# Linear attention plus SwiGLU on one core: tile 2 transposed by DMA, tile 0 normalised on ScalarE, and a new order of the first tiles

## The chip, the core and the metric

The kernel runs on one core of one Trainium2 chip. Time is device microseconds of one execution. The engines are named as in the profile: PE (TensorE, matrix multiplication), ACT (ScalarE), DVE (VectorE), POOL (GpSimd) and SP (SyncE, which here only issues DMAs). Each engine works through its own list in order and waits at semaphores for the others. A DMA is issued by SP or ACT and runs on the core's DMA engines.

## The reference, cut to what matters

S = 2048 rows, D = 512, F = 1792, 32 heads of 16, all tensors bf16.

```python
xn = layernorm(x)                                  # no scale or shift, eps 1e-5
q, k, v = split(xn @ wqkv)                         # 32 heads of 16
phi = lambda t: where(t > 0, t + 1, exp(t)) + 1e-6
kv = sum_s phi(k) v^T;  z = sum_s phi(k)           # per head
attn = (phi(q) kv) / (phi(q) z + 1e-6) @ wo
ffn = (silu(xn @ w_gate) * (xn @ w_up)) @ w_down
out = x + attn + ffn
```

The attention has no softmax. The kernel never forms v: it accumulates GT = xn^T phi(k) over all rows, and multiplies it by V's weights afterwards.

## The kernel before, in words

The 2048 rows are 16 tiles of 128. The kernel has two long stages. The first goes over the tiles: statistics of x, normalisation, a transpose of xn, the products with K's and Q's weights, phi(k), and the accumulation of GT in PSUM banks 4 to 7 (`gtacc`, four matmuls of 128x512 per tile). The second goes over 4 chunks of 512 rows times 14 slices of F (`ffn`), with the output rows (`outtile`) in between. K's product of tile t goes to bank 0 or 2, Q's to bank 1 or 3, by whether t is even.

The order of the work is written out by hand: `K.op` appends an instruction to the list of its engine, `K.dma` a transfer to the list of SP or ACT, and the waits follow from the names that each reads and writes. So the place of a line in the source is its place in its engine's list, and in no other.

Tiles 0 to 2 are treated apart, to start PE early. They are only centred (`xc_half`, DVE, two halves of 256 columns), transposed on PE (`tp_first`, two 128x128 transposes per half, evacuated to `xcT` by ACT at line 382), multiplied with K's and Q's weights (`proj_first`, in halves of two matmuls), and scaled by rstd only as ACT reads the products: `first_ek` (exp), `first_pk` (relu), `first_pq` (copy). For these tiles phi(k) is the sum of a clipped exponential and the relu, on POOL for tile 0 (`feat_pool`) and on DVE for tiles 1 and 2 (`first_feat`). GT needs the normalised rows as well, which `xn_dve` makes on DVE. The mean of tile 0 comes from DVE (`bns` and `agg`), that of tile 1 from ACT (`mean_act`, an activation whose sum is read out). Before the first tile, `fill` gives PE eight matmuls on a constant.

From tile 3 on, `xn_dve` makes xn, SP transposes it by DMA (`transpose_dma`), and `kproj` and `qproj` read the result.

`eps` and `rstd_of` make 1/sqrt(var + eps) from the variance, the second always on POOL. SP's list holds the loads of x, of the weights and the DMA transposes in one queue; at the start ACT issues three loads, too: x 1, one of four chunks of K's weights, and x 2.

Of the kernel before, what the change touches and what calls it, by code (L numbers as in the profile page):

```python
# [7 lines left out]
ALU = mybir.AluOpType  # L8
# [100 lines left out]
def bass_parallel_sum__linear_attn_block__swiglu_ffn__prompt_kernel(  # L109
# [16 lines left out]
    with contextlib.ExitStack() as es:  # L126
# [75 lines left out]
        def xload(eng, h, t0, n, after=()):  # L202
            K.dma(
                eng, lambda: h.dma_start(x_sb[:, t0:t0 + n, :], rows(xin, t0, n)),
                r=list(after), w=[("x", t0 + i) for i in range(n)],
            )

        def wqkv_load(eng, h, name, i, c0, n, after=()):
            K.dma(
                eng,  # L210
                lambda: h.dma_start(
                    wqkv_sb[:, c0:c0 + n, i * D:(i + 1) * D],
                    A_wqkv[c0 * P:(c0 + n) * P, i * D:(i + 1) * D].rearrange("(c p) f -> p c f", p=P),
                ),
                r=list(after), w=[(name, c) for c in range(c0, c0 + n)],
            )
# [32 lines left out]
        wqkv_load("sp", sp, "wk", 1, 0, 2)  # L249
        wqkv_load("act", act, "wk", 1, 3, 1)  # L250
        wqkv_load("sp", sp, "wk", 1, 2, 1)
        xload("act", act, 2, 1)
        xload("sp", sp, 3, 1)
        wqkv_load("sp", sp, "wq", 0, 0, 1)
        wqkv_load("sp", sp, "wq", 0, 1, 1)
        wqkv_load("sp", sp, "wq", 0, 2, 1)
        wqkv_load("sp", sp, "wq", 0, 3, 1)
        xload("sp", sp, 4, 1)
        xload("sp", sp, 5, 1)
        xload("sp", sp, 6, 2)  # L260

        cw = nc.const_aps.tensor(1.0, (P, P), bf)
        cx = nc.const_aps.tensor(1.0, (P, 512), bf)
# [1 line left out]
        def fill(n, cols, after=()):  # L265
            K.op(
                "pe",
                [
                    (lambda: pe.matmul(banks[3][:, 0:cols], cw, cx[:, 0:cols], start=True, stop=True))
                    for _ in range(n)  # L270
                ],
                r=list(after), w=[bk(3)],
            )
# [22 lines left out]
        def bns(t):  # L296
            K.op("dve", lambda: dve.bn_stats(stats[:, t, :], x_sb[:, t, :]), r=[("x", t)], w=[("st", t)])  # L297

        def agg(t):
            K.op("dve", lambda: dve.bn_aggr(mv[:, t, :], stats[:, t, :]), r=[("st", t)], w=[("mv", t)])  # L300

        def mean_act(t):
            K.op(
                "act",
                lambda: act.activation(
                    scr[:, :], x_sb[:, t, :], ACT.Copy, scale=1.0 / D, accum_out=mact[:, t, :],
                ),
                r=[("x", t)], w=[("mact", t), ("scr",)],
            )

        def xn_dve(t):
            K.op(
                "dve",
                lambda: dve.tensor_scalar(
                    out=xn_sb[:, t, :], in0=x_sb[:, t, :], scalar1=mv[:, t, 0:1], scalar2=rstd[:, t:t + 1],
                    op0=ALU.subtract, op1=ALU.mult,
                ),
                r=[("x", t), ("mv", t), ("rstd", t)], w=[("xn", t)],
            )

        def eps(t, eng):
            h = dve if eng == "dve" else pool
            K.op(
                eng,
                lambda: h.tensor_scalar(
                    out=vpe[:, t:t + 1], in0=mv[:, t, 1:2], scalar1=1e-5, scalar2=None, op0=ALU.add,
                ),
                r=[("mv", t)], w=[("vpe", t)],
            )

        def rstd_of(t):
            K.op(
                "pool",
                lambda: pool.tensor_tensor(out=rstd[:, t:t + 1], in0=vpe[:, t:t + 1], in1=nhalf[:, :], op=ALU.pow),
                r=[("vpe", t), ("nhalf",)], w=[("rstd", t)],
            )
# [19 lines left out]
        def xc_half(t, h, mean=None, dep="mv"):  # L356
            mean = mv[:, t, 0:1] if mean is None else mean

            K.op(
                "dve",  # L360
                lambda: dve.tensor_scalar(  # L361
                    out=xc_sb[:, t, h * HD:(h + 1) * HD], in0=x_sb[:, t, h * HD:(h + 1) * HD],
                    scalar1=mean, scalar2=None, op0=ALU.subtract,
                ),
                r=[("x", t), (dep, t)], w=[("xc", t, h)],
            )

        def tp_first(t, h, b):
            tb = banks[b].bitcast(bf)[:, 0:HD].rearrange("p (c s) -> p c s", c=2)
            K.op(  # L370
                "pe",
                [
                    (lambda c=c: pe.transpose(  # L373
                        tb[:, c, :], xc_sb[:, t, (2 * h + c) * P:(2 * h + c + 1) * P], ident[:, :],
                    ))
                    for c in range(2)
                ],
                r=[("xc", t, h), ("ident",)], w=[bk(b)],
            )
            K.op(  # L380
                "act",
                lambda: act.activation(xcT[:, NDC * t + 2 * h:NDC * t + 2 * h + 2, :], tb, ACT.Copy),  # L382
                r=[bk(b)], w=[("xcT", t, h)],
            )
# [22 lines left out]
        def proj_first(t, wname, h):  # L407
            lo, b = (D, kb(t)) if wname == "wk" else (0, qb(t))
            K.op(
                "pe",  # L410
                [
                    (lambda c=c: pe.matmul(  # L412
                        banks[b], xcT[:, NDC * t + c, :], wqkv_sb[:, c, lo:lo + D],
                        start=(c == 0), stop=(c == NDC - 1),
                    ))
                    for c in (2 * h, 2 * h + 1)
                ],
                r=[("xcT", t, h)] + [(wname, i) for i in ((2, 3) if h else (0, 1))], w=[bk(b)],
            )
# [55 lines left out]
        def first_pk(t):  # L475
            K.op(
                "act", lambda: act.activation(kpos[:, t, :], banks[kb(t)], ACT.Relu, scale=rstd[:, t:t + 1]),
                r=[bk(kb(t)), ("rstd", t)], w=[("kpos", t)],
            )
# [27 lines left out]
        def clip_k(t):  # L507
            clip(ek[:, t % NE, :], ("ek", t % NE))
# [47 lines left out]
            if t >= 3:  # L556
                transpose_dma(t)

        bns(0)
        mean_act(1)  # L560
        fill(8, 512)
        agg(0)
        eps(0, "pool")
        xc_half(0, 0)
        tp_first(0, 0, 4)
        xc_half(0, 1)
        tp_first(0, 1, 5)
        fill(1, P)
        xc_half(1, 0, mact[:, 1, :], "mact")
        tp_first(1, 0, 6)  # L570
        xc_half(1, 1, mact[:, 1, :], "mact")
        tp_first(1, 1, 7)
        bns(1)
        proj_first(0, "wk", 0)
        proj_first(0, "wk", 1)
        rstd_of(0)
        first_ek(0)
        first_pk(0)
        xn_dve(0)
        agg(1)  # L580
        eps(1, "pool")
        rstd_of(1)
        proj_first(1, "wk", 0)
        proj_first(1, "wk", 1)
        bns(2)
        proj_first(1, "wq", 0)
        first_ek(1)
        proj_first(0, "wq", 0)
        agg(2)
        xc_half(2, 0)  # L590
        tp_first(2, 0, 4)
        xc_half(2, 1)
        tp_first(2, 1, 5)
        clip_k(0)
        feat_pool(0)
        bns(3)
        agg(3)
        eps(3, "dve")
        rstd_of(3)
        bns(4)  # L600
        agg(4)
        proj_first(0, "wq", 1)
        first_pq(0)
        xn(3)
        xload("sp", sp, 8, 2)
        clip_k(1)
        xn_dve(1)
        proj_first(1, "wq", 1)
        first_pk(1)
        first_feat(1)  # L610
        first_pq(1)
        eps(4, "pool")
        rstd_of(4)
        xn(4)
        xload("sp", sp, 10, 2)
        bns(5)
        agg(5)
        eps(2, "pool")
        rstd_of(2)
        proj_first(2, "wk", 0)  # L620
        proj_first(2, "wk", 1)
        first_ek(2)
        clip_k(2)
        eps(5, "dve")
        rstd_of(5)
        xn_dve(2)
        first_pk(2)
        first_feat(2)
        proj_first(2, "wq", 0)
        proj_first(2, "wq", 1)  # L630
        first_pq(2)
        xn_dve(5)
        bns(6)
        agg(6)
        eps(6, "pool")
        gtacc(0)
        gtacc(1)
        kproj(3)
        exp_k(3)
        clip_k(3)  # L640
        maxadd_k(3)
        transpose_dma(5)
        xload("sp", sp, 12, 2)
        qproj(3)
        copy_q(3)
        exp_q(3)
        gtacc(2)
        rstd_of(6)
        zsum(0, 0)
        xn(6)  # L650
        xload("sp", sp, 14, 2)
        bns(7)
        agg(7)
        kproj(4)
        bns(8)
        exp_k(4)
        eps(7, "pool")
        rstd_of(7)
        qproj(4)
        exp_q(4)  # L660
        copy_q(4)
        clip_k(4)
        agg(8)
        eps(8, "pool")
        rstd_of(8)
        zsum(1, 1)
        maxadd_k(4)
        xn(7)
        stat(9)
        gtacc(3)  # L670

# [331 lines left out]
```

## Time and profile before

| | us |
|---|---|
| median of 3 runs | 211.75 (211.21 to 211.9) |
| the profiled execution | 211.24 |
| its span | 210.0 |
| PE busy | 206.7 |
| DVE busy | 119.9 |
| POOL busy | 74.3 |
| ACT busy | 70.2 |

The span runs from the first to the last recorded instruction; the profiled execution's own time has 1.24 us around it. Busy times are sums over instructions; matmuls are pipelined, so a matmul of 128x512 has a mean duration of 379 ns in the records though the next may start sooner. In a row of the timeline stand start, length, engine, line, operation, output and input, the count of merged instructions, and in brackets the idle time before the first with what ended it. A time to landing is from the issue of a DMA to its completion.

### The profile page before, as it was taken

Reading aid. Unit: us, or ns where it says so; the run is one execution under the profiler, and the core shown is the slowest. Engines: PE = TensorE matmul, PEld = TensorE weight load, DVE = VectorE, ACT = ScalarE, POOL = GpSimd, SP = SyncE. Lnnn points to the kernel's source line nnn. Section 1 sums busy time; section 2 is a strip of 40 time slices with the busy share of each in tenths; the row PEclk is TensorE's granted clock in tenths of the full one; section 3 lists DMA queues with packets and bytes.
Section 4 is the critical chain, followed back from the end, with each engine's and each line's share of the span. In section 5 each row is a group of like instructions: output and inputs, shape, how many; then the busy total and the mean of one; then the engine's idle time right before and its main releaser. Section 6 shows DMA issues by size and latency. Waiting matters only on the chain.

```text
span 210.0 us, 2773 instructions
## 1 busy us (share of the span) xinstructions
PE 206.7 (98%) x987; PEld 94.7 (45%) x987; DVE 119.9 (57%) x245; ACT 70.2 (33%) x124; POOL 74.3 (35%) x95
## 2 busy tenths in 40 slices
PE   7999999999999999999999999999999999999996
PEld 3444444445444444444444444444444444444444
DVE  3999998336265774647365746365556535374122
ACT  5876666956643331302122312213031213121000
POOL 3647997668032444222140432230424032221200
DMA  6666365696792011110202110202021010110201
GB/s 192 207 144 163 70 95 102 193 372 218 211 351 44 10 29 26 35 25 28 50 2 50 25 28 25 50 0 50 3 50 25 25 25 30 43 33 27 50 25 53
DMA packets 29743, 16.71 MB, mean 80 GB/s; under 512 B 20384, under 2 KB 29088, under 8 KB 29728
## 3 DMA queue, kind: packets, MB, share of 16 engines
q1 hardware_dynamic: 29296, 16.13, 28.9%
q10 hardware_dynamic: 432, 0.39, 0.6%
q8 instruction: 8, 0.13, 0.3%
q14 instruction: 7, 0.06, 0.1%
HBM read 9.70 MB, written 2.10 MB: 56 GB/s over the span
## 4 chain that ended last, share of the span: by engine, by line
PE 96%; DMA 1%; DVE 1%; ACT 0%; issue 0%
PE psum L723 46%; PE psum L906 23%; PE psum L398 11%; PE psum L895 7%; PE psum L539 7%; PE psum L412 2%; DMA x_sb<-in_A_x_dram 1%; ACT xcT L382 0%; PE psum L821 0%; PE psum L844 0%; DVE stats L297 0%; PE psum L373 0%; DVE xc_sb L361 0%; DVE out_sb L919 0%; DVE mv L300 0%
## 5 line engine op out<-in xcount | busy, mean ns | idle before, releaser
L738 ACT ACTIVATE sg<-psum 128x512 bf16<-128x512 f32 x56 | 33.4, 598 | 106.8 <-PE psum L723 103.8
L723 PE MATMUL psum<-xnT,wu_sb 128*128 128x512 bf16 x224 | 57.5, 379 | 0.0
L723 PE MATMUL psum<-xnT,wg_sb 128*128 128x512 bf16 x224 | 57.5, 379 | 0.0
L853 POOL TENSOR_TENSOR prod<-pkq,zb 128x512 f32<-128x512 bf16 x16 | 18.6, 1162 | 57.7 <-DVE pkq L463 57.7
L723 PEld LDWEIGHTS psum<-xnT,wu_sb 128*128 128x128 bf16 x224 | 21.9, 98 | 26.4
L723 PEld LDWEIGHTS psum<-xnT,wg_sb 128*128 128x128 bf16 x224 | 21.9, 98 | 26.2
L919 DVE TENSOR_TENSOR out_sb<-psum,x_sb 128x512 bf16<-128x512 f32 (+2 forms) x17 | 11.2, 660 | 36.2 <-PE psum L906 36.2
L877 POOL TENSOR_TENSOR pqn<-pkq,rden 128x512 bf16<-128x512 bf16 x16 | 16.9, 1055 | 36.6 <-DVE rden L871 36.6
L744 DVE TENSOR_TENSOR pkq<-psum,sg 128x512 bf16<-128x512 f32 x28 | 19.1, 687 | 18.5 <-PE psum L723 14.1
L744 DVE TENSOR_TENSOR xn_sb<-psum,sg 128x512 bf16<-128x512 f32 x28 | 18.8, 671 | 13.8 <-PE psum L723 12.2
L906 PE MATMUL psum<-wd_sb,xn_sb 128*128 128x512 bf16 (+2 forms) x126 | 25.7, 355 | 0.0
L906 PE MATMUL psum<-wd_sb,pkq 128*128 128x512 bf16 x112 | 25.5, 379 | 0.0
L398 PE MATMUL psum<-wqkv_sb,xnT 128*128 128x512 bf16 x104 | 24.4, 379 | 0.0
L531 POOL TENSOR_TENSOR zacc<-zacc,pkq 128x512 f32<-128x512 f32 x15 | 17.3, 1155 | 4.9 <-DVE ek L454 4.6
L906 PEld LDWEIGHTS psum<-wd_sb,xn_sb 128*128 128x128 bf16 x126 | 11.8, 98 | 12.4
L906 PEld LDWEIGHTS psum<-wd_sb,pkq 128*128 128x128 bf16 x112 | 11.0, 98 | 13.2
L895 PE MATMUL psum<-m_sb,eq 128*128 128x512 bf16 (+2 forms) x68 | 16.6, 367 | 0.0
L539 PE MATMUL psum<-pkq,xn_sb 128*128 128x512 bf16 x64 | 15.9, 379 | 0.0
L398 PEld LDWEIGHTS psum<-wqkv_sb,xnT 128*128 128x128 bf16 x104 | 10.1, 98 | 12.4 <-issue 0.5
L861 DVE TENSOR_REDUCE den<-prod 128x32 f32<-128x512 f32 x16 | 10.9, 684 | 5.7 <-POOL prod L853 5.7
L297 DVE BATCH_NORM_STATS2 stats<-x_sb 128x6 f32<-128x512 bf16 x16 | 10.9, 683 | 3.3 <-DMA x_sb<-in_A_x_dram 3.3
L463 DVE SCALAR_TENSOR_TENSOR pkq<-pkq,eq 128x512 bf16<-128x512 bf16 x16 | 11.1, 692 | 0.6
(62 smaller groups left out, 137.4 us busy)
## 6 DMA issues: line engine op xcount, KB each, us to landing
out_dram<-out_sb SPq DMA_DIRECT2D x15, 128.0 KB, 1.7
wg_sb<-in_B_w_gate_dram SPq DMA_DIRECT2D x2, 896.0 KB, 7.9
wu_sb<-in_B_w_up_dram SPq DMA_DIRECT2D x2, 896.0 KB, 6.0
wd_sb<-in_B_w_down_dram SPq DMA_DIRECT2D x1, 1792.0 KB, 9.8
x_sb<-in_A_x_dram SPq DMA_DIRECT2D x5, 256.0 KB, 2.9
wqkv_sb<-in_A_wqkv_dram SPq DMA_DIRECT2D x5, 128.0 KB, 3.9
x_sb<-in_A_x_dram SPq DMA_DIRECT2D x4, 128.0 KB, 3.4
wqkv_sb<-in_A_wqkv_dram SPq DMA_DIRECT2D x1, 512.0 KB, 7.9
```

Source lines behind the costliest of these rows:

```text
L398: (lambda c=c: pe.matmul(banks[b], xnT[:, c, t * P:(t + 1) * P], wqkv_sb[:, c, lo:lo + D], start=(c == 0), stop=(c == NDC - 1),))
L463: lambda: dve.scalar_tensor_tensor(out=dst, in0=src, scalar=0.0, in1=e, op0=ALU.max, op1=ALU.add,),
L531: lambda: pool.tensor_tensor(out=zacc[:, :], in0=zacc[:, :], in1=pk, op=ALU.add),
L539: (lambda c=c: pe.matmul(banks[4 + c], xn_sb[:, t, c * P:(c + 1) * P], pkq[:, t, 0, :], start=(t == 0), stop=(t == NT - 1),))
L723: (lambda c=c: pe.matmul(banks[b], w_sb[:, c, fc * P:(fc + 1) * P], xnT[:, c, C * 512:(C + 1) * 512], start=(c == 0), stop=(c == NDC - 1),))
L738: lambda: act.activation(sg[:, j % NSG, :], banks[gb], ACT.Silu),
L744: lambda: dve.tensor_tensor(out=hT(C, fc), in0=banks[ub], in1=sg[:, j % NSG, :], op=ALU.mult,),
L853: lambda: pool.tensor_tensor(out=p, in0=pkq[:, t, 1, :], in1=zb[:, :], op=ALU.mult),
L877: lambda: pool.tensor_tensor(out=pqn[:, t % NPN, :].rearrange("p (h e) -> p h e", e=DH), in0=pkq[:, t, 1, :].rearrange("p (h e) -> p h e", ...
L895: (lambda g=g: pe.matmul(dst, pqnT(t)[:, g, :], m_sb[:, g, lo:hi], start=(g == 0), stop=False,))
L906: (lambda fc=fc: pe.matmul(dst, hT(C, fc)[:, jj * P:(jj + 1) * P], wd_sb[:, fc, lo:hi], start=False, stop=(fc == NFC - 1),))
L919: lambda: dve.tensor_tensor(out=o, in0=src, in1=x_sb[:, t, lo:hi], op=ALU.add),
```

## The change

Nothing is computed differently but for where and when.

- Tile 2 is centred by one instruction of 512 columns (`xc_full`) and transposed by one DMA on SP (`transpose_xc`), in place of two halves, four PE transposes and two evacuations by ACT.
- Tile 0 is normalised by ACT (`xn_act`), with the scale rstd and the bias -mean * rstd that POOL makes (`negmean`), in place of `xn_dve(0)`.
- x 2 is loaded by SP behind K's weights, in place of ACT; x 3 comes behind two of Q's four chunks; x 6 and 7 behind the transpose of tile 2.
- The order of the first tiles is another. PE does all of K and Q of tiles 0 and 1, then GT of tile 0, then K and Q of tile 2, then GT of tile 1; before, tile 2's transposes came among Q of tiles 0 and 1, then K and Q of tile 2, then GT of tiles 0 and 1. The mean of tile 1 stands behind the first half of tile 0 in the source. Statistics and loads of tiles 3 to 8 are moved against each other.

```diff
@@ -249,15 +249,14 @@
         wqkv_load("sp", sp, "wk", 1, 0, 2)
         wqkv_load("act", act, "wk", 1, 3, 1)
         wqkv_load("sp", sp, "wk", 1, 2, 1)
-        xload("act", act, 2, 1)
-        xload("sp", sp, 3, 1)
+        xload("sp", sp, 2, 1)
         wqkv_load("sp", sp, "wq", 0, 0, 1)
         wqkv_load("sp", sp, "wq", 0, 1, 1)
+        xload("sp", sp, 3, 1)
         wqkv_load("sp", sp, "wq", 0, 2, 1)
         wqkv_load("sp", sp, "wq", 0, 3, 1)
         xload("sp", sp, 4, 1)
         xload("sp", sp, 5, 1)
-        xload("sp", sp, 6, 2)
 
         cw = nc.const_aps.tensor(1.0, (P, P), bf)
         cx = nc.const_aps.tensor(1.0, (P, 512), bf)
@@ -308,6 +307,25 @@
                 r=[("x", t)], w=[("mact", t), ("scr",)],
             )
 
+        def negmean(t):
+            K.op(
+                "pool",
+                lambda: pool.tensor_scalar(
+                    out=nb[:, t:t + 1], in0=mv[:, t, 0:1], scalar1=rstd[:, t:t + 1], scalar2=-1.0,
+                    op0=ALU.mult, op1=ALU.mult,
+                ),
+                r=[("mv", t), ("rstd", t)], w=[("nb", t)],
+            )
+
+        def xn_act(t):
+            K.op(
+                "act",
+                lambda: act.activation(
+                    xn_sb[:, t, :], x_sb[:, t, :], ACT.Identity, scale=rstd[:, t:t + 1], bias=nb[:, t:t + 1],
+                ),
+                r=[("x", t), ("nb", t), ("rstd", t)], w=[("xn", t)],
+            )
+
         def xn_dve(t):
             K.op(
                 "dve",
@@ -363,6 +381,22 @@
                     scalar1=mean, scalar2=None, op0=ALU.subtract,
                 ),
                 r=[("x", t), (dep, t)], w=[("xc", t, h)],
+            )
+
+        def xc_full(t):
+            K.op(
+                "dve",
+                lambda: dve.tensor_scalar(
+                    out=xc_sb[:, t, :], in0=x_sb[:, t, :], scalar1=mv[:, t, 0:1], scalar2=None, op0=ALU.subtract,
+                ),
+                r=[("x", t), ("mv", t)], w=[("xc", t, 0), ("xc", t, 1)],
+            )
+
+        def transpose_xc(t):
+            K.dma(
+                "sp",
+                lambda: sp.dma_start_transpose(out=xcT[:, NDC * t:NDC * (t + 1), :], in_=xc_sb[:, t, :]),
+                r=[("xc", t, 0), ("xc", t, 1)], w=[("xcT", t, 0), ("xcT", t, 1)],
             )
 
         def tp_first(t, h, b):
@@ -556,116 +590,112 @@
             if t >= 3:
                 transpose_dma(t)
 
-        bns(0)
-        mean_act(1)
         fill(8, 512)
-        agg(0)
-        eps(0, "pool")
+        stat(0)
         xc_half(0, 0)
         tp_first(0, 0, 4)
+        negmean(0)
+        fill(1, P)
+        mean_act(1)
         xc_half(0, 1)
         tp_first(0, 1, 5)
-        fill(1, P)
         xc_half(1, 0, mact[:, 1, :], "mact")
         tp_first(1, 0, 6)
         xc_half(1, 1, mact[:, 1, :], "mact")
         tp_first(1, 1, 7)
-        bns(1)
         proj_first(0, "wk", 0)
         proj_first(0, "wk", 1)
-        rstd_of(0)
         first_ek(0)
-        first_pk(0)
-        xn_dve(0)
+        bns(1)
         agg(1)
         eps(1, "pool")
-        rstd_of(1)
+        bns(2)
+        agg(2)
+        xc_full(2)
         proj_first(1, "wk", 0)
         proj_first(1, "wk", 1)
-        bns(2)
-        proj_first(1, "wq", 0)
+        first_pk(0)
+        rstd_of(1)
         first_ek(1)
+        clip_k(0)
         proj_first(0, "wq", 0)
-        agg(2)
-        xc_half(2, 0)
-        tp_first(2, 0, 4)
-        xc_half(2, 1)
-        tp_first(2, 1, 5)
-        clip_k(0)
         feat_pool(0)
         bns(3)
         agg(3)
         eps(3, "dve")
         rstd_of(3)
+        proj_first(1, "wq", 0)
+        xn_act(0)
+        proj_first(0, "wq", 1)
+        first_pq(0)
         bns(4)
         agg(4)
-        proj_first(0, "wq", 1)
-        first_pq(0)
-        xn(3)
-        xload("sp", sp, 8, 2)
+        eps(4, "pool")
+        proj_first(1, "wq", 1)
+        xn_dve(3)
         clip_k(1)
         xn_dve(1)
-        proj_first(1, "wq", 1)
+        gtacc(0)
+        transpose_xc(2)
+        proj_first(2, "wk", 0)
+        proj_first(2, "wk", 1)
+        xload("sp", sp, 6, 2)
+        proj_first(2, "wq", 0)
+        proj_first(2, "wq", 1)
         first_pk(1)
         first_feat(1)
-        first_pq(1)
-        eps(4, "pool")
+        gtacc(1)
         rstd_of(4)
-        xn(4)
-        xload("sp", sp, 10, 2)
+        xn_dve(4)
         bns(5)
         agg(5)
+        first_pq(1)
         eps(2, "pool")
         rstd_of(2)
-        proj_first(2, "wk", 0)
-        proj_first(2, "wk", 1)
         first_ek(2)
         clip_k(2)
         eps(5, "dve")
+        transpose_dma(3)
+        kproj(3)
+        qproj(3)
         rstd_of(5)
+        transpose_dma(4)
+        xload("sp", sp, 8, 2)
         xn_dve(2)
         first_pk(2)
         first_feat(2)
-        proj_first(2, "wq", 0)
-        proj_first(2, "wq", 1)
-        first_pq(2)
+        gtacc(2)
         xn_dve(5)
+        xload("sp", sp, 10, 2)
         bns(6)
+        exp_k(3)
+        clip_k(3)
         agg(6)
         eps(6, "pool")
-        gtacc(0)
-        gtacc(1)
-        kproj(3)
-        exp_k(3)
-        clip_k(3)
-        maxadd_k(3)
+        rstd_of(6)
         transpose_dma(5)
         xload("sp", sp, 12, 2)
-        qproj(3)
+        zsum(0, 0)
+        bns(7)
+        first_pq(2)
         copy_q(3)
-        exp_q(3)
-        gtacc(2)
-        rstd_of(6)
-        zsum(0, 0)
+        maxadd_k(3)
+        kproj(4)
         xn(6)
         xload("sp", sp, 14, 2)
-        bns(7)
+        exp_k(4)
+        qproj(4)
         agg(7)
-        kproj(4)
-        bns(8)
-        exp_k(4)
         eps(7, "pool")
+        exp_q(3)
         rstd_of(7)
-        qproj(4)
         exp_q(4)
         copy_q(4)
         clip_k(4)
-        agg(8)
-        eps(8, "pool")
-        rstd_of(8)
+        stat(8)
+        xn(7)
         zsum(1, 1)
         maxadd_k(4)
-        xn(7)
         stat(9)
         gtacc(3)
```

## The prediction

> **What bounds the kernel now.** I read the page's busy shares first, then the chain of work that ended last in order of time, then the timeline of the first 14 us, then single DMA issues with their time to landing.
>
> Busy shares, page of the kernel before:
>
> ```profile
> PE 206.7 (98%) x987; PEld 94.7 (45%) x987; DVE 119.9 (57%) x245; ACT 70.2 (33%) x124; POOL 74.3 (35%) x95
> ```
>
> TensorE (PE) is busy for nearly the whole span of 210.0 us. The chain (start, length, what) says from when:
>
> ```profile
> 4.44 0.30 PE psum L373 x2
> 4.76 0.61 ACT xcT L382 x2
> ...
> 5.57 0.41 ACT xcT L382
> ...
> 6.07 2.32 PE psum L412 x10
> 8.39 0.22 PE psum L373 x4
> 8.61 2.59 PE psum L412 x12
> 11.20 1.73 PE psum L539 x8
> ```
>
> From 6.07 us to the last output the chain is PE alone, 0.216 us per 128x512 matmul (2.59 / 12), without a gap. So the time is the moment at which the dense stream starts, plus its matmuls, plus any new wait in it. An engine other than PE matters only where it makes PE wait.
>
> The start, from the timeline (start, length, engine, line):
>
> ```profile
> 0.84 3.22 PE L269 MATMUL psum<-const-bfloat16-1.0 128*128 128x512 bf16 x8 [0.84 <-PEq L988]
> ...
> 3.49 0.63 ACT L305 ACTIVATE scr<-x_sb 128x512 bf16<-128x512 bf16 x1 [1.20 <-DMA x_sb<-in_A_x_dram]
> ...
> 4.02 0.19 ACT L305 ACTIVATION_READ_ACCUMULATOR scr<-x_sb 128x1 f32 x1
> ...
> 4.49 0.48 DVE L361 TENSOR_SCALAR xc_sb<-x_sb,mact 128x256 bf16<-128x256 bf16 x2
> ...
> 4.76 1.21 ACT L382 ACTIVATE xcT<-psum 128x256 bf16<-128x256 bf16 x4 [0.55 <-PE psum L373]
> ...
> 5.20 0.60 PE L412 MATMUL psum<-wqkv_sb,xcT 128*128 128x512 bf16 x2
> ...
> 8.04 1.15 POOL L496 TENSOR_TENSOR pkq<-kpos,ek 128x512 bf16<-128x512 f32 x1 [1.10 <-ACT kpos L477]
> ...
> 10.18 1.28 SPq L389 DMA_TRANSPOSE xnT<-xn_sb  x1
> ```
>
> The mean of tile 1 is taken on ScalarE (ACT) from 3.49 to 4.21 us, while ACT has nothing else to do: the first transposed half to evacuate exists only at 4.76. VectorE (DVE) therefore centres tile 1 at 4.49, directly behind tile 0, and PE does the first two K matmuls at 5.20.
>
> Two K matmuls later PE stands still until 6.07. The chain names ACT's evacuations, but the matmul at 6.07 needs only the second of four, which started at about 5.04 and takes 0.38. It also needs chunk 2 of K's weights. Issues around 1.74 us, KB each and us to landing:
>
> ```profile
> wqkv_sb<-in_A_wqkv_dram SPq DMA_DIRECT2D x1, 128.0 KB, 4.2
> x_sb<-in_A_x_dram ACTq DMA_DIRECT2D x1, 128.0 KB, 4.3
> ```
>
> The first is that chunk: issued at 1.74, landed at 5.96. The second is x 2 from ACT's queue at 1.83. So the start of the stream is now set by a weight transfer.
>
> **The change, part by part**
>
> *x 2 moves from ACT's queue to SP's, behind K's weights.* One issue of 0.45 leaves ACT and one enters SP, ahead of Q's four pieces; x 3 moves behind two of those. With x 2 no longer beside it, chunk 2 has one 128 KB piece less to share with. Three pieces (chunk 2, x 2, x 3) landed at 5.96, 6.13 and 6.34. [...] If nothing else changed, the stream would start up to 0.44 earlier, when PE is through with the two matmuls from 5.20 (5.63). The next part takes this away. x 2 itself lands by 6.3 and is now read at 7.1; x 3 by about 7.1, read at 8.6: both hidden.
>
> *The mean of tile 1 moves behind the first evacuation on ACT.* This decides. ACT works in order, and the first evacuation is put ahead of the mean. Evacuation at 4.76, next instruction 0.28 later (they started at 4.76 and 5.04): the mean begins at 5.04, takes 0.72 (3.49 to 4.21), ends at 5.76. Queued behind it on ACT: the second evacuation. Waiting for it: DVE's two halves of tile 1 (behind them, in order, all of DVE), and on PE the four transposes of tile 1, behind which stand the first K matmuls. DVE: halves at 5.78 and 5.98, the second done at 6.26 (0.28 each, 0.20 apart). PE: last time it went from the end of that half (4.97) to the first K matmul in 0.23 (5.20), so now 6.49, and 6.92 for the pair that started at 6.07. Loss at the start: **0.86**. The second evacuation, at about 5.76, and the chunk are there well before 6.92. Bounds: 0.75, if ACT overlaps the mean with the evacuation more than rows of one kind do, and 1.0, if the restart needs the 0.32 that lay between the first transpose (4.44) and its evacuation.
>
> *Four PE transposes of tile 2 go.* **-0.22**, the chain's row. Their two evacuations on ACT (0.27 each) and one of two DVE instructions go too; neither engine is the bound.
>
> *Order: all of Q 0, Q 1 and GT 0 come ahead of K 2.* Sixteen matmuls from 6.49 end at 9.95. GT 0 then needs K's features of tile 0 and tile 0 normalised. First exponential: 0.42 after the last K matmul starts (6.28 to 6.70), so 7.14 + 0.42 = 7.56; the relu follows 0.58 later at 8.14 and ends at 8.82; POOL's sum starts 0.08 later (7.96 to 8.04) and takes 1.15: 10.05, with GT 0 at about 10.14. Wait: **+0.19**. Bounds 0.05 and 0.4: POOL's durations are rough. DVE's clip comes between: mean of tile 1, K's statistics, statistics of tile 2 (0.73 + 0.22) and centring (0.33) put it at 8.4, done 8.7, before the relu is.
>
> *Tile 0 normalised on ACT.* One Identity of 128x512 from SBUF. No such row; between 0.53 (the mean's activation up to its read) and 0.69 (Identity from PSUM, L489). I take 0.63, the mean's own row, the same source and size. It starts at 9.30 behind the second exponential and ends at 9.93, just inside POOL's 10.05. If that cover goes it costs its excess over 10.05. It pushes the copy of Q 0 by 0.15, wanted only at 11.9. The new POOL scale (a 128x1 instruction, 0.22 to 0.32 by line 325) sits after tile 0's rstd, where POOL has nothing until tile 1's statistics at about 7.1: nothing; without that cover 0.3 before tile 1's exponential. DVE loses one normalisation of 0.33.
>
> *Tile 2 by DMA transpose.* Tile 2's centring on DVE ends at about 8.45, SP issues at 8.48. Landings of transposes here: 2.4 to 3.0, median 2.5, and 0.1 more to the matmul (5.96 to 6.07). At 8.48 the x loads are nearly through, so 2.5: K 2 can start at 11.08 and PE is through with GT 0 at 11.00. **+0.08**, bounds 0 and 0.55. SP then issues x 6 (moved from the opening to here, 0.57) and the transpose of tile 3. DVE has tile 3 normalised at about 11.0 (rstd behind POOL's sum: 10.57); issued 11.05, landed after 2.5 (as for the first transpose) to 3.0 (with x in flight, issued at 12.12), at 13.65 to 14.15 with the 0.1. PE has finished K 2, Q 2 and GT 1 at 13.67 (11.08 + 12 x 0.216). **+0.2**, between 0 and 0.5. x 8, now behind two transposes, is issued at about 13.8 and read about 18: hidden.
>
> Later GT, K and Q of tiles 2 to 7 have their inputs 0.7 or more ahead: GT 3 needs DVE's maximum at 17.5, PE is there at 18.3.
>
> Sum: 0.86 - 0.22 + 0.19 + 0.08 + 0.2 = **+1.1**. The profiled execution took 211.24 (span 210.0 and 1.24 around it), so 212.35. It lies 0.51 under the median of the runs shown, 211.75. If that spread is common to both kernels the median becomes 212.85; if it is the landing of chunk 2 (the gapless stream leaves little else inside the span), which the later start now covers, 212.35. I take the middle, **212.6**.
>
> [...] The granted clock reads 1.00 throughout, but the eight fill matmuls started 0.42 apart (first at 0.84, sixth at 2.92, seventh at 3.35), twice the 0.216 of later ones; the last came after 0.32, at 3.67. So PE was slow for about 2.7 us and then fast. The change leaves PE with eight transposes and one small fill between 4.05 and 6.49. [...]
>
> **Rivals**
> 1. *The clock falls back in the gap.* For: idle share. Against: transposes lie inside, and the clock held over 4.06 to 4.44. Another 2.7 us at 0.42 instead of 0.216 is 6.5 matmuls, +1.3, part of it absorbed by the waits of 0.47: 213.4 to 214.2.
> 2. *The transposes land in time or the spread hides the start.* The waits of tiles 0, 2 and 3 vanish, which leaves 0.86 - 0.22 = +0.64 on 211.24: 211.9, and 212.3 where the larger figures hold. If the runs before differed by the landing of chunk 2 (211.75 then means 6.47), this is within 0.3% of their median. For: the uncertain 0.2 s are each a difference of two large sums. Against: tile 0's wait hangs on POOL's 1.15, the same for every such row.
> 3. *Faster.* The earlier weights decide: PE restarts at 5.63 and drops the transposes, -0.44 - 0.22, so 210.6, or 211.1 with the spread. It decides where tile 1's mean costs PE nothing, that is done by about 4.5, as before. For: DMA set the start until now. Against: ACT's order has the mean behind an evacuation that can't start before tile 0's statistics (3.15 to 4.06), centring and transposes; or chunk 2 lands after 7.1 in the runs before, which would put them at 212.4, above all three shown.
>
> **How the numbers follow.** Forecast case 0.6, at 212.3 to 212.9; rival 1 0.12; rival 2 0.2; rival 3 0.08. 0.3% is 0.64 us, about what a measurement of this kernel can tell from no change, so slower begins at 212.39. From the forecast case 0.02 falls under that; slower 0.7, same 0.22, faster 0.08. Range 211.8 to 214.1: it leaves out rival 3 and the ends of rival 1.
>
> **What would show it.** In the profile after: the mean's activation at about 5.0 behind one evacuation; DVE idle from 4.6 to 5.8; first K matmul near 6.5; no matmul pair of K 0 waiting for weights; GT 0 near 10.1, released by POOL; K 2 near 11.1 and K 3 near 13.9, both after a transpose; from there a gapless stream. Wrong if the mean runs before 4.8, if matmuls past 6.5 are 0.42 apart, or if K 2 waits a microsecond for its transpose.

## The result, and the profile after

The changed kernel took 212.68 us (median of 13 runs, 212.21 to 214.13), the kernel before 211.53 (13 runs, 210.91 to 212.01). The ratio is 1.0072, 95% interval 1.0056 to 1.0089: slower by 0.7%, where 212.6 was forecast with 211.8 to 214.1 as its range.

The 13 runs fall into two groups: seven at 212.21 to 212.68 and six at 213.19 to 214.13. The first profile taken, 214.13 with a span of 212.8, is the slowest of them. Its page has

```profile
span 212.8 us, 2763 instructions
...
PE 208.9 (98%) x983; PEld 95.3 (45%) x983; DVE 119.5 (56%) x243; ACT 70.3 (33%) x123; POOL 74.4 (35%) x96
```

PE is the bound as before, with four matmuls less. Its start, from the timeline of the same profile:

```profile
0.84 3.57 PE L268 MATMUL psum<-const-bfloat16-1.0 128*128 128x512 bf16 x8 [0.84 <-PEq L1018]
...
4.87 0.38 ACT L416 ACTIVATE xcT<-psum 128x256 bf16<-128x256 bf16 x1 [2.58 <-PE psum L407]
...
5.15 0.62 ACT L304 ACTIVATE scr<-x_sb 128x512 bf16<-128x512 bf16 x1
...
5.67 0.19 ACT L304 ACTIVATION_READ_ACCUMULATOR scr<-x_sb 128x1 f32 x1
...
5.89 0.48 DVE L379 TENSOR_SCALAR xc_sb<-x_sb,mact 128x256 bf16<-128x256 bf16 x2 [1.32 <-ACT scr L304]
...
6.64 5.40 PE L446 MATMUL psum<-wqkv_sb,xcT 128*128 128x512 bf16 x16
...
11.88 1.03 PE L573 MATMUL psum<-pkq,xn_sb 128*128 128x512 bf16 x4
```

The mean stands behind one evacuation, DVE is idle for 1.32 until it is there, and the first K matmul comes at 6.64. What the forecast case did not have: the 16 matmuls of K and Q take 5.24 (6.64 to 11.88) instead of 3.46. Up to about 10.05 they start 0.42 apart.

A later profile of the same kernel (212.42, span 211.2; the run e9 below) belongs to the lower group:

```profile
6.03 0.48 PE L407 MATMUL psum<-ident,xc_sb 128*128 128x128 bf16 x4 [1.09 <-DVE xc_sb L379]
...
6.35 3.62 PE L446 MATMUL psum<-wqkv_sb,xcT 128*128 128x512 bf16 x16
...
8.75 1.15 POOL L530 TENSOR_TENSOR pkq<-kpos,ek 128x512 bf16<-128x512 f32 x1 [0.80 <-ACT kpos L511]
...
9.13 0.82 ACT L323 ACTIVATE xn_sb<-x_sb,nb,rstd 128x512 bf16<-128x512 bf16 x1
...
10.05 1.02 PE L573 MATMUL psum<-pkq,xn_sb 128*128 128x512 bf16 x4
...
10.91 1.89 PE L446 MATMUL psum<-wqkv_sb,xcT 128*128 128x512 bf16 x8
12.64 1.03 PE L573 MATMUL psum<-pkq,xn_sb 128*128 128x512 bf16 x4
...
23.00 1.03 PE L573 MATMUL psum<-pkq,xn_sb 128*128 128x512 bf16 x4
24.36 1.89 PE L432 MATMUL psum<-wqkv_sb,xnT 128*128 128x512 bf16 x7 [0.34 <-ACT pkq L481]
```

Here all K and Q matmuls are 0.216 apart, and two waits are left: GT 0 at 10.05, where PE was ready at 9.81 (6.35 + 16 x 0.216), and K of tile 7 at 24.36, where PE was ready at 23.87 (23.00 + 4 x 0.216). The row names ACT, but tile 7's transpose landed last. Its issue in e9, in the timeline of SP and then in the list of DMA issues with us to landing:

```profile
19.60 1.19 SPq L423 DMA_TRANSPOSE xnT<-xn_sb  x1
```
```profile
xnT<-xn_sb SPq DMA_TRANSPOSE x1, 4.6
```

So it landed at 24.2, after 4.6 where the others of these first tiles took 2.4 to 3.4. In the first profile it was issued at 21.23, took 4.6 as well, and K of tile 7 waited from 25.69 to 25.99. Term by term against the kernel before, in us (the first row puts the second pair two steps of 0.216 behind the first K matmul; what the slow steps of the first profile add stands in the second row):

| term | forecast | e9 | first profile |
|---|---|---|---|
| second pair of K 0, at 6.07 before | +0.86 | +0.71 (6.78) | +1.00 (7.07) |
| matmuls 0.42 apart | 0 | 0 | +1.78 (11.88 against 6.64 + 3.46) |
| PE transposes of tile 2 | -0.22 | -0.22 | -0.22 |
| wait of GT 0 | +0.19 | +0.24 | 0 |
| waits of K 2 and K 3 | +0.28 | 0 | 0 |
| wait of K of tile 7 | 0 | +0.49 | +0.30 |
| sum | +1.1 | +1.2 | +2.9 |
| span less 210.0 | | +1.2 | +2.8 |

### The profile page after: what moved, and what is told of

It is laid out like the page before. It is cut to its first block, busy times and chain, and to the rows that moved or that the text cites. A ratio compares the mean times of both kernels' runs of the same rounds, so it can differ in the third digit from the quotient of the medians.

```text
span 212.8 us, 2763 instructions
## 1 busy us (share of the span) xinstructions
PE 208.9 (98%) x983; PEld 95.3 (45%) x983; DVE 119.5 (56%) x243; ACT 70.3 (33%) x123; POOL 74.4 (35%) x96
## 4 chain that ended last, share of the span: by engine, by line
PE 95%; DMA 2%; DVE 1%; ACT 1%; issue 0%; ACTq 0%
PE psum L753 45%; PE psum L936 23%; PE psum L432 9%; PE psum L925 6%; PE psum L573 5%; PE psum L446 3%; DMA xnT<-xn_sb 2%; PE psum L268 2%; PE psum L407 0%; PE psum L851 0%; PE psum L874 0%; ACT scr L304 0%; DVE stats L296 0%; ACT ek L469 0%; ACT xcT L416 0%
## 5 line engine op out<-in xcount | busy, mean ns | idle before, releaser
L753 PEld LDWEIGHTS psum<-xnT,wu_sb 128*128 128x128 bf16 x224 | 21.9, 98 | 26.4
L753 PEld LDWEIGHTS psum<-xnT,wg_sb 128*128 128x128 bf16 x224 | 21.9, 98 | 26.2
```

Source lines behind the costliest of these rows:

```text
L753: (lambda c=c: pe.matmul(banks[b], w_sb[:, c, fc * P:(fc + 1) * P], xnT[:, c, C * 512:(C + 1) * 512], start=(c == 0), stop=(c == NDC - 1),))
```

## The experiments

The theory (A): the mean's place costs the start about 1 us, and the gap that it leaves on PE keeps PE's clock slow in some executions; all else is small. Rival B: the order behind it costs. Rival C: the slow clock comes whatever the gap. What is measured of a slow clock is the distance between the starts of 128x512 matmuls, 0.42 in the first profile up to 10.05 and 0.216 in e9; the granted clock reads 1.00 in both. That a clock stands behind the distance is the author's reading.

**e1: the mean first again, all else changed.**

```diff
+        mean_act(1)
         fill(8, 512)
         ...
         fill(1, P)
-        mean_act(1)
```

> The changed kernel with one line moved back: ACT takes the mean of tile 1 before the first evacuation, as in the kernel before; all the rest of the change stays. Theory A (the mean's place delays PE's first K matmul by about 1 us, and the gap it leaves keeps PE's clock slow in some executions; the rest of the change is small): first K matmul at about 5.2, the second pair at about 5.6 without a wait for weights (chunk 2 landed at 4.9 in the changed kernel), all at 0.216; waits of 0.2 each at GT 0, K 2, K 3; in sum 0.1 to 0.5 below the kernel before, and no executions 0.8 above the lowest. Rival B (the order behind it costs: DMA transpose, normalisation on ACT, GT 0 ahead of K 2): stays 0.7 to 1.2 above the kernel before. Rival C (the slow clock comes with any execution, whatever the gap): executions spread over 1.5 us as those of the changed kernel.

Measured: 211.36 against 211.46, ratio 1.000 (0.9987 to 1.0012), highest of 12 executions 212.04. So moving that one line back removes the whole loss: B falls. But the gain of 0.1 to 0.5 that A had expected is not there either, though PE is through with its first K matmuls early. PE in this kernel:

```profile
5.19 2.76 PE L446 MATMUL psum<-wqkv_sb,xcT 128*128 128x512 bf16 x12
8.15 1.04 PE L446 MATMUL psum<-wqkv_sb,xcT 128*128 128x512 bf16 x4 [0.20 <-DMA wqkv_sb<-in_A_wqkv_dram]
...
23.16 1.89 PE L432 MATMUL psum<-wqkv_sb,xnT 128*128 128x512 bf16 x7 [0.16 <-DMA xnT<-xn_sb]
```

The gain of 0.44 (no wait after the first pair) and 0.22 is given back at Q's last weights (8.15 instead of 5.19 + 12 x 0.216 = 7.78: 0.37) and at the transpose of tile 7 (0.32, landed after 4.6).

**e2 and e11: the kernel before with the mean late.**

```diff
-        mean_act(1)
         fill(8, 512)
         ...
         tp_first(0, 0, 4)
+        mean_act(1)
```

> The kernel before with that one line alone moved: the mean of tile 1 behind the first evacuation on ACT. Theory A: first K matmul at 6.5 to 6.65 in place of 5.20, the pair behind it at 6.9 to 7.1 in place of 6.07: 0.8 to 1.0 above the kernel before with a fast clock, up to 1.8 more with a slow one, so a median of +0.9 to +1.9. Rival B: within 0.3 of the kernel before. Rival C: +0.9, with a spread as of the kernel before.

> The kernel before with the mean of tile 1 behind the first evacuation, once more, for the count of executions in its two groups (four of eight lay at 213.5 to 214.0, four at 212.1 to 212.3). Theory A (PE's idle gap leaves the clock to chance): again both groups, 30 to 60 in 100 above 213.2. Rival C (the upper group was chance of that hour): at most one in ten above 213.2.

Measured: 1.0068 (1.0043 to 1.0094) with four executions at 212.09 to 212.26 and four at 213.50 to 213.96, and later 1.0048 (1.0024 to 1.0071) with nine at 211.81 to 212.28 and three at 213.00 to 213.77. Of these last twelve two lie above 213.2, fewer than the 30 to 60 in 100 that A expected and more than C's one in ten: both groups came again, but their shares are not settled. The profile of e2 (212.09):

```profile
6.09 0.48 PE L373 MATMUL psum<-ident,xc_sb 128*128 128x128 bf16 x4 [1.16 <-DVE xc_sb L361]
6.41 2.75 PE L412 MATMUL psum<-wqkv_sb,xcT 128*128 128x512 bf16 x12
```

First K matmul at 6.41, its second pair at 6.84 instead of 6.07: 0.77; the span is 0.9 longer. One line alone makes the loss of the whole change, and both groups.

**e3: the loads alone.**

```diff
-        xload("act", act, 2, 1)
-        xload("sp", sp, 3, 1)
+        xload("sp", sp, 2, 1)
         wqkv_load("sp", sp, "wq", 0, 0, 1)
         wqkv_load("sp", sp, "wq", 0, 1, 1)
+        xload("sp", sp, 3, 1)
```

> The kernel before with the loads alone changed: x 2 on SP behind K's weights, x 3 behind two of Q's pieces. Theory A (the start of the kernel before was set by the landing of K's chunk 2 at 5.96): the chunk lands at about 4.9 as in the changed kernel, the pair at 6.07 starts at 5.63, and the time falls by 0.3 to 0.5. Rival: something else is late (the evacuations that the chain names end at 5.98), the pair stays at about 6.0, within 0.15 of the kernel before.

Measured: 211.26 against 211.46, ratio 0.9998 (0.9981 to 1.0014): no difference. In its profile K's first two chunks landed after 4.2 (at about 5.5, against 3.2 and 4.4 before), the third after 4.2 (5.9), and the first K matmul waited until 5.63. Over all profiles the third chunk took 3.2, 3.5, 4.2, 3.4, 3.5, 3.7, 3.4, 3.7 with x 2 behind it on SP, and 4.2, 3.6, 4.1, 4.1, 4.2, 3.6 with x 2 on ACT: means of 3.6 and 4.0. The move seems worth some 0.4 on that landing, but landings differ by 1.0 from one execution to the next.

**e4: the change with matmuls in the gap.**

```diff
         tp_first(0, 1, 5)
+        fill(3, 512)
```

> The changed kernel with three more matmuls on a constant (128x512) on PE, in the gap in which it waits for tile 1's mean; their results are read by nobody. Theory A: PE is busy from 4.4 to 6.2, so the clock is fast by the first K matmuls in every execution; these start at 6.5 to 6.7 as before, 0.216 apart; the executions lie at 212.1 to 212.6 and the group above 213 is gone. Rival C (the clock's moment has nothing to do with the gap): the same two groups as the changed kernel, median 212.7, some 6 in 13 above 213.

Measured: 1.0062 (1.0048 to 1.0076), six executions at 212.48 to 213.21, in one group, but higher than the 212.1 to 212.6 expected. In its profile the first matmuls were not slow (13 of K and Q from 7.15 in 2.97, 0.216 apart); a transpose issued at 17.90 landed after 4.3 instead, and K of tile 6 waited from 21.43 until 22.28, 0.85. So the median (212.82) is not lower than without the matmuls.

**e5 and e12: the mean late in the kernel before, with matmuls in the gap.** The edit of e2 with that of e4.

> The kernel before with the mean of tile 1 moved behind the first evacuation, and three matmuls on a constant put into the gap that this leaves on PE (their results are read by nobody). Without them the executions fell into two groups, 212.1 to 212.3 and 213.5 to 214.0. Theory A (PE's idle gap decides whether its clock is fast at the first K matmul): one group, 212.0 to 212.5, 0.7 to 1.0 above the kernel before, none above 213. Rival (the moment at which the clock gets fast has nothing to do with the gap): both groups again, about half above 213.4.

> The same with three matmuls on a constant in PE's gap, once more (one of six lay above 213, at 213.5). Theory A: at most one in six above 213.2, lower group at 212.1 to 212.9 (one transpose's wait of 0.55 in it). Rival C: the same share above 213.2 as without the matmuls.

Measured: 1.0061 (1.0038 to 1.0085) with executions at 212.13, 212.32, 212.33, 212.74, 212.85 and 213.52, then 1.0036 (1.0012 to 1.0060) with twelve at 212.11 to 212.97. The first set had one execution in the upper group, which A had not expected. Counting all: without matmuls in the gap (the changed kernel, e2, e9, e11) 14 of 39 executions took 213.0 or more; with them (e4, e5, e10, e12) 2 of 25. With the mean first, 0 of 24 did in e1 and e3, and 1 of 22 of the kernel before in the last set of runs. These kernels are faster by about 0.9 to begin with, so 213.0 is a higher bar for them; at 212.4, about 1.0 above their median, it is 1 of 24 and 3 of all 94 executions of the kernel before. So with the gap the upper group is more frequent, but the gap isn't its only cause, and the share changed between sets of runs: 10 of 21 in the changed kernel's first set and e2, 4 of 18 in e9 and e11.

**e8: the price of the slow clock.**

```diff
-        fill(8, 512)
+        fill(2, 512)
```

> The kernel before with two opening fill matmuls instead of eight: PE idle from about 1.7 to 4.4. It measures the price of the slow clock by itself. Theory A (the clock follows PE's recent work): K and Q matmuls from 5.2 on start 0.42 apart for about 2.7 to 3.5 us in every execution, the time is 1.0 to 1.8 above the kernel before, in one group. Rival (the clock gets fast at some moment whatever PE did): within 0.3 of the kernel before.

Measured: 1.0067 (1.0041 to 1.0092), executions at 212.26, 212.47, 213.12 and 213.21. The profile (212.47) has the mean first and no late input:

```profile
0.84 1.01 PE L269 MATMUL psum<-const-bfloat16-1.0 128*128 128x512 bf16 x2 [0.84 <-PEq L988]
4.43 0.61 PE L373 MATMUL psum<-ident,xc_sb 128*128 128x128 bf16 x4 [2.58 <-DVE xc_sb L361]
...
5.37 4.30 PE L412 MATMUL psum<-wqkv_sb,xcT 128*128 128x512 bf16 x12
9.51 0.39 PE L373 MATMUL psum<-ident,xc_sb 128*128 128x128 bf16 x4
```

Twelve matmuls in 4.14 instead of 2.59 (12 x 0.216): 1.55, of which the wait for weights would have hidden 0.44. So in this profile less work on PE in the first 5 us (two fills in 1.01 instead of eight in 3.22) went with first matmuls 0.345 apart on the mean (4.14 / 12).

**e6: is the late transpose a fetch of PE's instructions?** In e1, e2, e4, the kernel before and both profiles of the change, the transpose that took 4.3 to 4.6 was in flight when the DMA's instruction queue q8 moved a packet of 0.02 MB; in e5, e7, e10 and e11 it was so as well (4.1 to 4.4). In e3, e8 and e12 the packet fell on the issue of a transpose, which took 2.8 to 3.2. No transpose of any profile took more than 3.6 without such a packet in flight. q8 has 8 of them for PE's 1974 matmuls and weight loads, which is why the author takes them for fetches of PE's instructions.

The edit, on top of e1's:

```diff
-        fill(8, 512)
+        fill(32, P)
```

> The changed kernel with the mean first, and its eight opening fill matmuls of 512 columns replaced by 32 of 128 columns: the same PE time, 48 instructions more on PE. Theory: in all runs so far one transpose landed after 4.3 to 4.6 instead of 2.5 just where queue q8 of the DMA fetched PE's instructions (at 20 us in this kernel with eight fills, tile 7, 0.32 of waiting on PE). With 48 instructions more the fetch comes 4 to 6 us earlier, at 14 to 17; the transpose in flight then (tile 5 or 6) lands after 4 or more, tile 7's after 2.4 to 3.1, and PE's wait moves to that tile, up to 0.9. Rival (the load of x 14 just ahead of tile 7's transpose slows it): tile 7's transpose again takes 4.3 to 4.6, and the time is that of the kernel with eight fills.

Measured: the window from 15 to 16 us of this kernel, queues and then the transposes of tile 5 and tile 7 (issued at 14.26 and 18.68):

```profile
q8 instruction: 1, 0.02, 6.4%
...
xnT<-xn_sb SPq DMA_TRANSPOSE x1, 4.0
```
```profile
xnT<-xn_sb SPq DMA_TRANSPOSE x1, 3.0
```
```profile
18.30 1.90 PE L432 MATMUL psum<-wqkv_sb,xnT 128*128 128x512 bf16 x8 [0.22 <-DMA xnT<-xn_sb]
```

The fetch moved from 20.9 (e1) to 15.7, about what 24 more matmuls with their weight loads take at 0.216 each (5.2). The long landing moved with it from tile 7 to tile 5, and PE waits at tile 5 and no more at tile 7. The rival, the load of x 14 ahead of it, falls. By way of a late transpose the fetch cost PE 0.30 to 0.85 in eight of the fourteen profiles, and nothing in the other six. Counting alone doesn't give the moment of a fetch: with two fills instead of eight (e8) it came at 23.8 instead of 27.7, though PE's list is shorter, and two executions of one kernel differ by 2.2 (28.1 in e2 and 25.9 in e11; 21.9 in e5 and 24.1 in e12). So the same kernel may pay this wait in one execution and not in the next: e5's profile (212.74) lost 0.71 at tile 7, e12's (212.11) nothing. The time of e6 was 211.82 (1.0023, 1.0006 to 1.0041), above e1; in its profile the wait for Q's last piece was 0.15 longer.

**e7: Q's weights ahead of x 3, with the mean first.**

```diff
-        xload("sp", sp, 3, 1)
         wqkv_load("sp", sp, "wq", 0, 2, 1)
         wqkv_load("sp", sp, "wq", 0, 3, 1)
+        xload("sp", sp, 3, 1)
```

> The changed kernel with the mean first and, in addition, x 3 behind all four pieces of Q's weights instead of behind two. In the kernel with the mean first PE waited 0.37 at 8.15 for Q's last piece. Theory: the piece lands 0.4 earlier, PE doesn't wait there, GT 0 starts near 8.7 or waits for POOL until 8.9, and the time falls by 0.15 to 0.4 to 0.1 to 0.5 below the kernel before. Rival (another input is due next: GT 0's features, tile 2's transpose, or tile 3's statistics behind the later x 3): a new wait of the same size, time unchanged within 0.15.

Measured: 211.82 against 211.35, ratio 1.0019 (1.0007 to 1.0031): slightly slower, a miss. The wait for Q's weights is not gone. Q's last piece was issued 0.49 earlier than in e1, but landed after 3.9 instead of 3.5, so that the matmul that needs it started at 8.12, where PE was ready at 7.86: a wait of 0.26 in place of 0.37. PE's weight loads show it (the view of the matmuls merges this gap into one row):

```profile
8.09 0.56 PEld L446 LDWEIGHTS psum<-wqkv_sb,xcT 128*128 128x128 bf16 x4 [0.56 <-DMA wqkv_sb<-in_A_wqkv_dram]
```

GT 0 follows at 8.98 without a wait of its own. Two waits are new: GT 1 at 11.74 (ready at 11.58), and K of tile 3, whose transpose was issued at 10.59 instead of 9.75:

```profile
13.12 1.89 PE L432 MATMUL psum<-wqkv_sb,xnT 128*128 128x512 bf16 x8 [0.34 <-DMA xnT<-xn_sb]
```

PE was ready for it at 12.60: 0.52 lost, far more than the 0.1 won. K of tile 7 waited 0.41, where e1 has 0.32.

**e9: the changed kernel again.**

> The changed kernel as it is, for more executions and a second profile: in the first one PE's clock was slow for the first K and Q matmuls. Theory A: the executions again form two groups, 212.2 to 212.7 and 213.2 to 214.1, each with a third or more of them; a profile from the lower group has the first K matmul at 6.4 to 6.7 and the next ones 0.216 apart, GT 0 near 10.2, and a wait of 0.3 to 0.9 at one transpose between 17 and 24 us where PE's instructions are fetched. Rival C (slow clock and gap unrelated): a spread without a gap in the middle.

Measured: 212.52 (1.0066, 1.0046 to 1.0086), five executions at 212.39 to 212.68 and one at 213.45: both groups, but fewer in the upper one than the third expected. In its profile, shown above, the first K matmul came at 6.35, GT 0 at 10.05, and the wait at a transpose was 0.49.

**e10: tile 0 normalised on DVE, in e4's kernel.**

```diff
         xc_full(2)
+        xn_dve(0)
         ...
-        xn_act(0)
```

> The changed kernel with the three fill matmuls in PE's gap, and tile 0 normalised on DVE behind the centring of tile 2 instead of on ACT. With ACT, GT 0 started at 10.21, 0.09 behind the end of ACT's activation (9.30 + 0.82) and 0.15 behind the end of POOL's sum (8.91 + 1.15). Theory (ACT's activation ends last by a little): GT 0 at 10.1 to 10.2, released by POOL, a gain of 0 to 0.1. Rival (DVE's extra 0.33 delays the clip and so POOL): GT 0 at 10.3 or later.

Measured, in a single execution: K 0 at 6.45, so PE is ready for GT 0 at 9.91, and GT 0 starts at 10.25, a wait of 0.34 against 0.24 in e4 (6.51, 10.21). POOL's sum begins at 8.95, released by the clip on DVE, which the extra normalisation pushed to 8.51. So GT 0 lies between the two forecasts, but what delayed it is what the rival said, by 0.1: ACT was not the worse place, even at 0.82.

No kernel tried is faster than the kernel before beyond the noise; e1 and e3 equal it within 0.2%.

## Why the prediction was right

**The mean behind the evacuation: right.** Its working gave 6.49 for the first K matmul and 0.86 of loss. Measured were 6.35 in e9 (a loss of 0.71, but with x 0's statistics done 0.26 earlier than in the profile before, so 0.97 on equal terms), 6.51 in e4 and 6.64 in the first profile (1.00, at the upper bound). e2 shows that this line alone makes the loss, e1 that without it there is none. The second evacuation and the weights were there, as said.

**The loads: right on the average, not in each execution.** An earlier landing of chunk 2 was to bring the start forward by up to 0.44; against 5.96 before it landed at 4.96 in the first profile, 1.0 earlier, at 5.9 in e3, and 0.4 earlier on the average of all profiles. e3 shows that this is no gain to count on: the landings of K's weights differ by 1.0 between executions. With the late mean none of it matters.

**PE transposes: right,** 0.22.

**GT 0: right in size, wrong in its releaser.** 0.24 for 0.19. The Identity was taken at the mean's 0.63 with 0.69 as the upper bound; it took 0.80 to 0.82 and ended at 9.95, just after POOL's 9.90. The bound from nearest rows did not hold what a new form cost. The three differ in more than their source: the mean's activation takes no operand per row, the Identity from PSUM one (the scale), the new one two (scale and bias). That this makes the difference was not tested.

**Tile 2 and tile 3 by transpose: mis-sized by 0.28.** Both landed after 2.4 to 2.5 in e9 and PE did not wait; the value for tile 3 had been raised for x loads in flight.

**"Later GT, K and Q of tiles 2 to 7 have their inputs 0.7 or more ahead": this step failed.** It took 2.4 to 3.0 as the range of a transpose. The trace of before had one of 4.5, issued at 25.20 for a tile that had time to spare; the working left it out. Its row in the list of issues, and the queue from 27 to 28 us, while it was in flight:

```profile
xnT<-xn_sb SPq DMA_TRANSPOSE x1, 4.5
```
```profile
q8 instruction: 1, 0.02, 6.1%
```

The instruction fetch hit tile 7 and cost 0.49 in e9, 0.30 in the first profile. That the sum of +1.1 came out at +1.2 in e9 was luck in part: this 0.49 stands against 0.28 that tiles 2 and 3 did not cost and a start that was 0.15 earlier than forecast.

**The clock: the price was named, the way to it and its chance were not right.** Rival 1 had 0.12; 7 of 19 executions of the changed kernel lie at 213.19 or more, four of them in rival 1's 213.4 to 214.2. The prediction's own sign of being wrong, matmuls past 6.5 that are 0.42 apart, is there in the first profile, whose span is 2.8 longer instead of 1.1. Rival 1 took PE's clock for fast before the gap, as in the profile before, where the last fills come faster. In eleven of the thirteen profiles with the full opening fill it was still slow at its end (3.57 throughout, against 3.22 before and 3.18 in e2). So the first profile does not show a fall in the gap: the fills ahead of it are as far apart as the K and Q matmuls behind it, about 0.42, and 0.216 comes only after 10.05. No profile shows matmuls slowed by a gap that were fast before it: in e2, where the fills were fast at their end and PE's last idle time in the gap was 1.16, the twelve matmuls behind it took 2.75, 0.216 apart. Only one execution of the upper group was profiled, so that all of it is the clock rests on that profile and on e8.

**The median: near by luck.** The lower group lies where the sum said (212.35 against 212.21 to 212.68). The 0.25 on top of it stood for a spread of the kernel before; what lifted the median to 212.68 was the upper group, which is the slow clock's as far as it was profiled.

## What to carry to other kernels

Where one engine runs without a gap to the end, look for what sets its first dense instruction, and read each engine's list in order there: here a line that was harmless in an idle slot held up ACT, DVE and PE one slot later, by 0.71 to 1.00. With the late start some executions paid a second price, matmuls 0.42 apart instead of 0.216 and 1.78 in the one that was profiled; it shows as two groups of times and not in the profile of the lower one (e9). An edit that wins at the start meets the next input that was just in time: a gain of 0.66 ended as none (e1), and a further one of 0.1 as a loss (e7).

## What the runs showed of the hardware

One packet of 0.02 MB on queue q8, taken for a refill of PE's instructions, went with landings of 4.0 to 4.6 us instead of 2.5 for the DMA transpose in flight in the first 30 us, in eleven of the fourteen profiles (2.8 to 3.2 in the other three), and PE waited up to 0.85 where a tile had less than that in hand. The moment from which matmuls of 128x512 start 0.216 apart instead of 0.42 differs between executions: with the same eight fills it came at about 3.5 us in the profile before, after 4.4 but before 6.4 in e9, and at about 10 in the first profile after. The granted clock reads 1.00 in all three; only the distance between matmuls shows it. An Identity of 128x512 bf16 from SBUF with scale and bias per row took 0.80 to 0.82 on ACT, against 0.69 from PSUM with a scale alone.
